# Attention with a routed expert layer on one core: transposing transfers ahead of pair loads on SyncE's queue, and products with V side by side

## The chip, the cores and the metric

The kernel runs on one core of one Trainium2 chip. The metric is device time in microseconds (us) from launch to end. Three runs of the kernel before gave 577.92, 581.92 and 582.97 us; their median is 581.92. Everything read from a trace comes from one profiled execution, which took 580.57 us and whose span from the first to the last instruction is 578.8 us.

## What is computed

Attention over 4 batches, 8 heads, 576 positions and 64 columns a head, with an additive bias that depends on the positions, then an expert layer in which each token goes to one of 8 experts.

```python
scores = scale * np.matmul(q, k.transpose(0, 1, 3, 2))
h = np.maximum(x @ w1 + b1, 0.0)          # x: 576 x 576 position ratios
bias = h @ w2                             # one 576 x 576 plane a head
scores = scores + bias.transpose(2, 0, 1)[None, :, :, :]
scores = scores - np.max(scores, axis=-1, keepdims=True)
attn = np.exp(scores)
attn = attn / (np.sum(attn, axis=-1, keepdims=True) + 1e-09)
attn_out = np.matmul(attn, v)
...
logits = np.einsum('bsd,de->bse', x, w_gate)   # x: attn_out, heads side by side
h = np.maximum(x[b, s] @ w1[e], 0.0)
out[b, s] = p[e] * (h @ w2[e])
```

## The kernel before

Two heads of one batch make a pair. There are 16 pairs (`pairs`, four head pairs p by four batches b), numbered here 0 to 15 in the order in which they run. Pairs 0 to 3 run while the bias planes are still being made; pairs 4 to 15 run one behind the other. A pair is worked in five blocks of query rows (`QORD` = 1, 2, 0, 3, 4), and a block of 128 rows in two units, one a head; the last block, of 64 rows, is one unit for both heads. So a pair has nine units, and unit u is a position in one list of events.

A unit (`emit_s`) makes a score plane on TensorE (L305, L306: the query in 16 bits against the high and the low half of the key), adds the bias and takes the minimum on VectorE (L325), and takes the exponential on ScalarE (L330). Before the product with V the exponentials have to be transposed. That goes two ways:

- For pairs 4 to 12 (`DMP`) the first two blocks are split into a high and a low 16-bit half: ScalarE casts (L336), VectorE subtracts (L346, in `emit_lo`), and a DMA turns the whole 128 x 2304 tile into `eT` (L350). There are two such transposing transfers a pair, called T1 (first block) and T2 (second block) here. `av_split` then makes the products with V, in three parts: part 0 (L363 and eight of L369) reads what both T1 and T2 brought, parts 1 and 2 are eight and eight more of L369.
- All other blocks are transposed on TensorE (L398) and copied out of PSUM (L404, L415).

VectorE's subtraction and its copies, the casts of V (L276, with a POOL subtraction behind each), the output rows (`emit_rows`: transposes L456, a scaling L468, a 16-bit cast `xo` L482 on ScalarE, its low half on POOL or VectorE) and their stores (`store_rows`, L492 and L495) lie between.

Loads: `load_pair` (L141, L143 twice, L145) brings query, key halves and V of the pair after the next one, 288 to 320 KB each, and POOL splits them into 16-bit halves (L122, L119). `load_bias` (L166 to L168 for a full block) reads the bias planes of the next head pair back from DRAM. All of them, T1, T2 and the row stores are issued by SyncE (SP), one behind the other: an instruction there that waits holds all that stand behind it. `xo` has one buffer, so the cast of a pair's rows waits until the rows before are stored.

What sets the order: each step has a key, a unit number plus a fraction (`at(u + ..., ...)`), and the steps are recorded by key. Every engine but SyncE is then ordered by a scheduler from what was recorded; in the stretch of pairs 4 to 12, SyncE keeps the recorded order word for word (`manual_schedule`). The keys that matter: a unit's work at u; T1 at the third unit of a pair and T2 at its fifth (`unit_r` at u + 0.1, which issues row stores first); the pair load at the first unit (inside `prefetch`); the bias read-backs at the fifth unit, ahead of T2; row stores `LST` = 5 units after the rows were made; `av_split`'s three parts 5.8, 8.55 and 8.8 units behind the second block's first head's end (`LA0`).

Of the kernel before, what the change touches and what calls it, by code (L numbers as in the profile page):

```python
# [21 lines left out]
NQ = 5  # L22
NP = H // 2
# [26 lines left out]
def build(tc, nc, io):  # L50
# [214 lines left out]
    dmx = ExitStack()  # L265
    dbox = {}
    pend, ucur = [], [0]
    stores, LST = [], 5

    def prefetch(gi):  # L270
        p, b, qt = groups[gi]
        if (p, b) in DMP and qt == QORD[0]:
            if "e" not in dbox:
                open_right()
            v16 = dbox["v"].tile([128, 2, NQ, 128], F16, name="v16")
            nc.vector.tensor_copy(out=v16[:, 0], in_=v_t[b, p])  # L276
            sub_pool(v16[:, 1], v_t[b, p], v16[:, 0])
            v16_t[p, b] = v16
        if p == 0:
            if G0 - 6 <= gi < G0 - 1:  # L280
                load_bias(1, QORD[gi - G0 + 6])
            if G0 - 6 <= gi < G0 - 4:
                load_pair(gi - (G0 - 6), 1, wr_t[KORD[-1]])
        else:
            if qt == QORD[0]:
                nx = gi // NQ + 2
                if nx < len(pairs):
                    load_pair(pairs[nx][1], pairs[nx][0])
            if p + 1 < NP and qt == QORD[2]:
                for x in (((0, 1), (2,), (3,), (4,)) if p < NP - 2 else ((0, 1, 2), (3, 4), (), ()))[b]:  # L290
                    load_bias(p + 1, QORD[x])

    def emit_s(u):
        gi, hh = units[u]
# [343 lines left out]
    bias_step(12)  # L638
    LB0, LC0, LO0 = 3.2, 6, 1.28
    LTS = (3.2, 3.2, 2.95, 3.2, 3.95)  # L640
    LA0, LAN, LA1, LL, LOUT = (5.8, 8.55, 8.8), 10.62, (6.35, 6.6), 8.6, 8.72
    NU = len(units)
    ex_t = {}

# [396 lines left out]
            bias_step(BSTEP[s])  # L1041

    def unit_r(s):
        while stores and stores[0][0] <= s:
            store_rows(*stores.pop(0)[1:])
        while pend and pend[0][0] < s:
            emit_lo(pend.pop(0)[1])

    def unit_x(s):
        for st in steps:  # L1050
# [26 lines left out]
    def at(key, f, *a):  # L1077
        ev.append((key, len(ev), partial(f, *a)))

    for u in range(NU):  # L1080
# [3 lines left out]
        at(u + 0.1, unit_r, u)  # L1084
        at(u + (LB0 if p == 0 else LTS[QORD.index(qt)]), emit_t, u)
        at(u + 0.4, unit_x, u)
        if qt == QORD[1] and hh == 1:
            if (p, b) in DMP:
                for n in range(3):
                    at(u + LA0[n], av_split, p, b, n)  # L1090
            elif p:
                at(u + LAN, emit_av, p, b, 0)
            else:
                at(u + LC0 + 0.6, emit_av, p, b, 0)
# [430 lines left out]
```

## Time and profile before

| | |
|---|---|
| median of three runs | 581.92 us (577.92 to 582.97) |
| the profiled execution | 580.57 us, span 578.8 us |
| TensorE matmul busy | 529.8 us, 92% of the span |
| VectorE busy | 470.5 us, 81% |
| ScalarE busy | 437.1 us, 76% |
| GpSimd (POOL) busy | 263.2 us, 45% |
| mean granted TensorE clock | 0.978 of full speed |
| HBM read, written | 128.92 MB, 20.80 MB |

How to read it: a busy share is an average over stages with different limits. Score reads of pair 4 begin at about 127 us and those of pair 13 at about 277 us; the first 127 us are the bias planes with pairs 0 to 3, the stretch from 340 us on is the expert layer. The change touches the stretch between 127 and 277 us above all. A row of the timeline merges like instructions that follow each other; the bracket gives the idle time before and what ended it. SyncE's rows give the time that an issue took, not the transfer.

### The profile page before, as it was taken

To read this page: it belongs to the slowest core of one execution; us is meant where nothing else is said; L and a number is where in the kernel's file an instruction comes from. 1 tells how busy PE (TensorE), PEld (TensorE's weight loads), DVE (VectorE), ACT (ScalarE), POOL (GpSimd) and SP (SyncE) were. 2 spreads that over 40 slices of the span, in tenths; PEclk is the share of its full clock that TensorE was granted. 3 is DMA by queue.
4 is the path that set the end of the run, shared out by engine and by line. 5 is a ranking of instruction groups with operands and counts; after the bars stand their busy time and mean duration, and the time that the engine had idled before them with its cause. 6 is when DMAs were issued, how large, how long until landed. Compare 5 with 4: busy or idle time off the path is not lost. (4 is left out here: it accounts for less than half of the span.)

```text
span 578.8 us, 14244 instructions
## 1 busy us (share of the span) xinstructions
PE 529.8 (92%) x5310; PEld 355.9 (61%) x5310; DVE 470.5 (81%) x915; ACT 437.1 (76%) x743; POOL 263.2 (45%) x293
## 2 busy tenths in 40 slices
PE   5669999989979999998999998999999999999992
PEld 1124445766646667766576776587676867777851
DVE  6989885688778898899788458789999799897950
ACT  5879876867878887887589874468998787986940
POOL 5200000894299958967646660522424354344111
PEclk9899999999989999999799999899999999999997
DMA  8766546857798799749174001776899947887250
GB/s 281 259 186 185 144 132 189 267 147 155 192 238 224 190 264 242 198 104 261 33 252 134 22 22 35 257 236 211 271 266 301 333 136 213 160 217 230 18 185 30
DMA packets 104285, 107.33 MB, mean 185 GB/s; under 512 B 71565, under 2 KB 80911, under 8 KB 100114
## 3 DMA queue, kind: packets, MB, share of 16 engines
q1 hardware_dynamic: 99424, 90.63, 56.5%
q0 software_dynamic: 4640, 15.43, 8.8%
q8 instruction: 44, 0.72, 0.5%
q10 hardware_dynamic: 146, 0.30, 0.2%
q14 instruction: 31, 0.25, 0.1%
HBM read 128.92 MB, written 20.80 MB: 259 GB/s over the span
## 5 line engine op out<-in xcount | busy, mean ns | idle before, releaser
L325 DVE CUSTOM_DVE_ANT_0 e<-sps,wb 128x576 f32<-128x576 f32 x144 | 106.8, 747 | 20.0 <-PE sps L306 15.0
L330 ACT ACTIVATE e<-e,st 128x576 f32<-128x576 f32 x144 | 111.5, 775 | 14.2 <-DVE st L325 12.7
L917 DVE TENSOR_TENSOR w<-wb,w 128x2048 bf16<-128x2048 f32 (+1 forms) x36 | 72.3, 2052 | 2.0 <-ACT w L910 2.0
L305 PE MATMUL sps<-kh,qs 128*128 128x288 f16 x256 | 69.5, 293 | 3.3 <-DVE st L325 2.8
L1014 POOL DMA_INDIRECT out_dram<-y,odx x17 | 32.2, 1892 | 88.8 <-ACT y L1004 48.8
L404 ACT COPY eT<-ta 128x512 f32<-128x512 f32 x92 | 52.6, 581 | 23.5 <-PE ta L398 16.6
L398 PE MATMUL ta<-c_cpb,e 128*128 128x128 f32 x432 | 68.1, 278 | 2.0 <-ACT eT L404 1.1
L306 PE MATMUL sps<-kl,qs 128*128 128x288 f16 x256 | 69.2, 291 | 0.0
L988 PE MATMUL yp<-w,hhT 128*128 128x512 bf16 (+1 forms) x272 | 64.9, 381 | 1.1 <-ACT w L910 1.1
L910 ACT CAST w<-wb 128x2048 f16<-128x2048 f32 (+1 forms) x40 | 63.8, 1640 | 2.2 <-DMA wb<-in_w_dram 2.2
L211 PE MATMUL sps<-hd,c_cpa 128*32 128x512 f32 (+17 forms) x352 | 48.3, 505 | 15.1 <-DVE hd L197 10.3
L949 PE MATMUL sps<-xT,we 128*128 128x128 f16 (+1 forms) x1056 | 61.3, 219 | 1.0 <-DVE we L917 1.0
L949 PEld LDWEIGHTS <-we 128*128 128x128 f16 (+1 forms) x1056 | 59.9, 98 | 3.5 <-DVE we L917 1.1
L398 PEld LDWEIGHTS ta<-c_cpb,e 128*128 128x128 f32 x432 | 50.1, 141 | 12.7 <-ACT e L330 2.6
L428 PE MATMUL av<-eT,vt 128*64 128x320 f32 (+1 forms) x368 | 57.7, 425 | 0.0
L197 DVE TENSOR_SCALAR hd<-tab,bp 128x448 f32<-128x448 f32 (+17 forms) x130 | 50.2, 445 | 3.9 <-PE sps L211 3.8
L917 DVE TENSOR_TENSOR we<-ws,we 128x2048 bf16<-128x2048 f32 (+1 forms) x25 | 49.0, 1993 | 2.7 <-ACT we L910 2.6
L949 PEld LDWEIGHTS <-wb 128*128 128x128 f16 (+1 forms) x1056 | 46.9, 98 | 2.8 <-issue 1.5
L949 PE MATMUL sps<-xT,wb 128*128 128x128 f16 (+3 forms) x1056 | 48.5, 207 | 0.0
L988 PEld LDWEIGHTS <-hhT 128*128 128x128 f16 x272 | 25.9, 99 | 30.3 <-issue 2.8
L910 ACT CAST we<-ws 128x2048 f16<-128x2048 f32 (+1 forms) x26 | 41.4, 1637 | 2.1 <-DMA ws<-in_w_dram 2.1
L119 POOL TENSOR_TENSOR qs<-qf,qs 64x288 f16<-64x288 f32 x48 | 40.9, 871 | 1.7
(234 smaller groups left out, 1008.7 us busy)
## 6 DMA issues: line engine op xcount, KB each, us to landing
ws<-in_w_dram SPq DMA_DIRECT2D x34, 1024.0 KB
wb<-in_w_dram SPq DMA_DIRECT2D x34, 1024.0 KB
hs<-in_w_dram SPq DMA_DIRECT2D x20, 1024.0 KB
bias_d<-bv SPq DMA_DIRECT2D x36, 295.5 KB
kf<-in_kt_dram SPq DMA_DIRECT2D x24, 288.0 KB
wb<-bias_d SPq DMA_DIRECT2D x16, 288.0 KB
wb<-bias_d SPq DMA_DIRECT2D x16, 256.0 KB
xrow_d<-xo SPq DMA_DIRECT2D x16, 256.0 KB
```

The lines of the kernel that those rows point to most:

```text
L197: nc.vector.tensor_scalar(out=hd[:, 0:n], in0=tab[:, 0:n], scalar1=bp[:, k:k + 1], scalar2=0.0, op0=ALU.add, op1=ALU.max,)
L305: nc.tensor.matmul(out=ps[:, half, 0:288], lhsT=lq, rhs=kh[:, j], start=True, stop=False)
L306: nc.tensor.matmul(out=ps[:, half, 0:288], lhsT=lq, rhs=kl[:, j], start=False, stop=True)
L325: nc.vector.tensor_tensor_reduce(out=e, in0=ps[:, :, 0:288], in1=bsl, scale=-0.125, scalar=1e30, op0=ALU.add, op1=ALU.min, accum_out=st[:, ...
L330: nc.scalar.activation(out=e, in_=e, func=AF.Exp, scale=-1.0, bias=st[:, 0:1], accum_out=sm)
L398: nc.tensor.transpose(out=ta[:, j, :], in_=e[:, o:o + 128], identity=ident)
L404: nc.scalar.copy(out=eTv[:, :, hh, o:o + 128], in_=ta)
L428: nc.tensor.matmul(out=av[64 * x:64 * x + 64, 0:n], lhsT=vt[:, j, 64 * x:64 * x + 64], rhs=eT[:, 2 * j + x, 0:n], start=False, stop=(j == 3),)
L910: nc.scalar.copy(out=wh[c][:, sl], in_=src)
L917: nc.vector.tensor_tensor(out=wl[c][:, sl], in0=src, in1=wh[c][:, sl], op=ALU.subtract)
L949: nc.tensor.matmul(out=hp.rearrange("p a j -> p (a j)")[:, n * f:n * f + n], lhsT=w[f // 4][:, o:o + 128], rhs=x[:, kt], start=(i == 0), s ...
L988: nc.tensor.matmul(out=yp, lhsT=x[:, kt], rhs=w[kt // 4][:, 512 * (kt % 4):512 * (kt % 4) + 512], start=(i == 0), stop=(i == len(terms) - 1),)
```

## The change

Names of constants move (`LST`, `LBI`, `LPD`, `LPN`, `LPX`), and these keys with them:

- `load_pair` leaves `prefetch` and becomes a step of its own, `load_ahead`. For the first six pairs of the stretch (pairs 4 to 9, `DMP[0:LPX]`) its key is 4.15 units behind the pair's first unit, which is behind T2; for the others it is 0.01 ahead of the first unit.
- the bias read-backs (`load_next_bias`) get key 4.2 instead of 4.0, behind T2 and behind the pair load;
- row stores come one unit later (`LST` 6), and within a unit behind the transposing transfers, not ahead of them;
- `av_split`'s parts get 7.2, 8.0 and 8.02 instead of 5.8, 8.55 and 8.8: part 0 later, parts 1 and 2 earlier and one directly behind the other.

No instruction is added or taken away on the compute engines, and no transfer.

```diff
--- before.py
+++ after.py
@@ -265,7 +265,7 @@
     dmx = ExitStack()
     dbox = {}
     pend, ucur = [], [0]
-    stores, LST = [], 5
+    stores = []
 
     def prefetch(gi):
         p, b, qt = groups[gi]
@@ -281,14 +281,16 @@
                 load_bias(1, QORD[gi - G0 + 6])
             if G0 - 6 <= gi < G0 - 4:
                 load_pair(gi - (G0 - 6), 1, wr_t[KORD[-1]])
-        else:
-            if qt == QORD[0]:
-                nx = gi // NQ + 2
-                if nx < len(pairs):
-                    load_pair(pairs[nx][1], pairs[nx][0])
-            if p + 1 < NP and qt == QORD[2]:
-                for x in (((0, 1), (2,), (3,), (4,)) if p < NP - 2 else ((0, 1, 2), (3, 4), (), ()))[b]:
-                    load_bias(p + 1, QORD[x])
+
+    def load_ahead(gi):
+        nx = gi // NQ + 2
+        if nx < len(pairs):
+            load_pair(pairs[nx][1], pairs[nx][0])
+
+    def load_next_bias(p, b):
+        if p + 1 < NP:
+            for x in (((0, 1), (2,), (3,), (4,)) if p < NP - 2 else ((0, 1, 2), (3, 4), (), ()))[b]:
+                load_bias(p + 1, QORD[x])
 
     def emit_s(u):
         gi, hh = units[u]
@@ -638,7 +640,9 @@
     bias_step(12)
     LB0, LC0, LO0 = 3.2, 6, 1.28
     LTS = (3.2, 3.2, 2.95, 3.2, 3.95)
-    LA0, LAN, LA1, LL, LOUT = (5.8, 8.55, 8.8), 10.62, (6.35, 6.6), 8.6, 8.72
+    LA0, LAN, LA1, LL, LOUT = (7.2, 8.0, 8.02), 10.62, (6.35, 6.6), 8.6, 8.72
+    LST, LBI = 6, 4.2
+    LPD, LPN, LPX = 4.15, -0.01, 6
     NU = len(units)
     ex_t = {}
 
@@ -1041,10 +1045,10 @@
             bias_step(BSTEP[s])
 
     def unit_r(s):
+        while pend and pend[0][0] < s:
+            emit_lo(pend.pop(0)[1])
         while stores and stores[0][0] <= s:
             store_rows(*stores.pop(0)[1:])
-        while pend and pend[0][0] < s:
-            emit_lo(pend.pop(0)[1])
 
     def unit_x(s):
         for st in steps:
@@ -1084,6 +1088,9 @@
         at(u + 0.1, unit_r, u)
         at(u + (LB0 if p == 0 else LTS[QORD.index(qt)]), emit_t, u)
         at(u + 0.4, unit_x, u)
+        if p and hh == 0 and qt == QORD[0]:
+            at(u + (LPD if (p, b) in DMP[0:LPX] else LPN), load_ahead, gi)
+            at(u + LBI, load_next_bias, p, b)
         if qt == QORD[1] and hh == 1:
             if (p, b) in DMP:
                 for n in range(3):
```

Three places show what it does to the order. Line numbers of the changed kernel are two higher in these places.

SyncE, from the row stores in pair 5 on; `e_1933` and `e_1967` are the tiles of T1 and T2 of pair 5, `qf`, `kf`, `vt` are the load of pair 7, `wb_126` the read-back of a bias block. Before:

```order
L492 DMA xrow_d<-xo 128x4x128
L495 DMA xrow_d<-xo 64x128
L492 DMA xrow_d<-xo 128x4x128
L495 DMA xrow_d<-xo 64x128
L141 DMA qf<-in_qt_dram 128x576
L143 DMA kf<-in_kt_dram 128x576 x2
L145 DMA vt<-in_vl_dram 128x640
L350 DMA_TRANSPOSE eT<-e_1933 128x18x128
L166 DMA wb_126<-bias_d 128x576
L167 DMA wb_126<-bias_d 128x512
L168 DMA wb_126<-bias_d 128x64
L350 DMA_TRANSPOSE eT<-e_1967 128x18x128
```

and in the changed kernel, where the same two tiles are named `e_1898` and `e_1952`:

```order
L494 DMA xrow_d<-xo 128x4x128
L497 DMA xrow_d<-xo 64x128
L494 DMA xrow_d<-xo 128x4x128
L497 DMA xrow_d<-xo 64x128
L352 DMA_TRANSPOSE eT<-e_1898 128x18x128
L352 DMA_TRANSPOSE eT<-e_1952 128x18x128
L141 DMA qf<-in_qt_dram 128x576
L143 DMA kf<-in_kt_dram 128x576 x2
L145 DMA vt<-in_vl_dram 128x640
L166 DMA wb_126<-bias_d 128x576
L167 DMA wb_126<-bias_d 128x512
L168 DMA wb_126<-bias_d 128x64
```

The load of four transfers and the three read-backs, which stood ahead of T1 and between T1 and T2, now stand behind both; the two row stores still stand ahead of T1.

VectorE, at the same place: `e_1933` and `e_1967` as above, `xo` the low half of the rows whose store is the second pair of `xrow_d` rows above; each pair of ISA rows is one unit's score read. Before:

```order
L125 TENSOR_TENSOR xo<-xr,xo 128x5x128
L382 COPY xt<-av 128x256
L415 COPY eT<-tb_r 128x64
L325 ISA e,st<-sps,wb_127 128x576
L325 ISA st 128x1
L346 TENSOR_TENSOR e_1933<-e,e_1933 128x1152
L325 ISA e,st<-sps,wb_127 128x576
L325 ISA st 128x1
L325 ISA e,st<-sps,wb_127 128x576
L325 ISA st 128x1
L346 TENSOR_TENSOR e_1967<-e,e_1967 128x1152
L442 COPY xt<-av 128x320
```

and in the changed kernel:

```order
L348 TENSOR_TENSOR e_1898<-e,e_1898 128x1152
L327 ISA e,st<-sps,wb_127 128x576
L327 ISA st 128x1
L327 ISA e,st<-sps,wb_127 128x576
L327 ISA st 128x1
L125 TENSOR_TENSOR xo<-xr,xo 128x5x128
L327 ISA e,st<-sps,wb_127 128x576
L327 ISA st 128x1
L444 COPY xt<-av 128x320
L348 TENSOR_TENSOR e_1952<-e,e_1952 128x1152
L446 COPY sums<-av 64x2
```

T1's subtraction moved ahead by one score read, and the `xo` subtraction went from ahead of both to between them.

TensorE, in pair 6, around the products of pair 5 (`v_1898` before, `v_1886` now, is V of pair 5 in 16 bits). Before, these rows hold no product with V; the first of them, L363, comes behind sixteen more rows:

```order
L414 MATMUL tb_r<-c_cpb,e 128x128
L305 LDWEIGHTS qs
L305 MATMUL sps<-kh,qs 128x288
L306 LDWEIGHTS qs
L306 MATMUL sps<-kl,qs 128x288
L305 LDWEIGHTS qs
L305 MATMUL sps<-kh,qs 128x288
L306 LDWEIGHTS qs
L306 MATMUL sps<-kl,qs 128x288
L398 MATMUL ta<-c_cpb,e 128x128 x4
L305 LDWEIGHTS qs
```

and in the changed kernel, from the same `tb_r` row on:

```order
L416 MATMUL tb_r<-c_cpb,e 128x128
L307 LDWEIGHTS qs
L307 MATMUL sps<-kh,qs 128x288
L308 LDWEIGHTS qs
L308 MATMUL sps<-kl,qs 128x288
L365 LDWEIGHTS v_1886
L365 MATMUL av<-eT,v_1886 128x256
L365 LDWEIGHTS v_1886
L365 MATMUL av<-eT,v_1886 128x256
L365 LDWEIGHTS v_1886
L365 MATMUL av<-eT,v_1886 128x256
```

Part 0 of `av_split` moved ahead by two and a half score planes here, although its key is later: the scheduler sets what it takes to be ready.

## Rows read from the trace of the kernel before

**Rows 1.** Windows view: us, busy of each engine, PEclk, DMA share, GB/s

```profile
127.00:277.00 150.00, 138.77 (x1186) 96.01 (x1185) 128.88 (x332) 119.67 (x277) 112.49 (x127) 0.98 0.81 203
```

**Rows 2.** Waits view of PE, 125 to 285 us: total us, times, longest

```profile
PE av L363 <- DMA eT<-e: 6.0, 3, 3.4
```

**Rows 3.** Timeline of PE: start us, us, line, operation [idle before <-what ended it]

```profile
147.39 0.49 PE L363 MATMUL av<-eT,v 128*128 128x256 f16 x3 [1.39 <-DMA eT<-e]
...
160.96 0.29 PE L306 MATMUL sps<-kl,qs 128*128 128x288 f16 x1
...
166.76 0.49 PE L363 MATMUL av<-eT,v 128*128 128x256 f16 x3 [3.35 <-DMA eT<-e]
...
222.32 1.30 PE L536 MATMUL av<-c_cpb,xt 128*128 128x32 f32 x10 [1.40 <-DVE sums L444]
...
272.67 0.50 PE L363 MATMUL av<-eT,v 128*128 128x256 f16 x3 [1.21 <-DMA eT<-e]
...
273.56 0.51 PE L684 MATMUL sps<-ident,fk 128*16 128x128 f16 x5 [0.16 <-DVE fk L608]
```

**Rows 4.** Windows view of PE alone: busy us, PEclk, DMA share, GB/s

```profile
168.17:171.58 3.41, 3.41 (x19) 0.50 0.50 118
...
273.98:277.39 3.41, 3.07 (x19) 0.50 0.47 146
277.39:280.80 3.41, 3.41 (x21) 0.50 0.30 87
```

**Rows 5.** Timeline of SyncE's queue: start us, us taken to issue, line

```profile
140.43 4.83 SPq L350 DMA_TRANSPOSE eT<-e  x1
...
151.59 0.58 SPq L141 DMA_DIRECT2D qf<-in_qt_dram  x1
...
153.22 0.37 SPq L145 DMA_DIRECT2D vt<-in_vl_dram  x1
153.70 4.51 SPq L350 DMA_TRANSPOSE eT<-e  x1
158.26 0.57 SPq L166 DMA_DIRECT2D wb<-bias_d  x1
...
159.88 3.27 SPq L350 DMA_TRANSPOSE eT<-e  x1
...
248.95 1.77 SPq L350 DMA_TRANSPOSE eT<-e  x1
250.81 0.53 SPq L492 DMA_DIRECT2D xrow_d<-xo  x1
251.40 0.56 SPq L495 DMA_DIRECT2D xrow_d<-xo  x1
```

**Rows 6.** Timeline of DVE around pairs 5 and 9

```profile
149.75 0.82 DVE L125 TENSOR_TENSOR xo<-xr,xo 128x640 bf16<-128x640 f32 x1
...
152.19 1.35 DVE L346 TENSOR_TENSOR e<-e,e 128x1152 f16<-128x1152 f32 x1
...
154.82 1.35 DVE L346 TENSOR_TENSOR e<-e,e 128x1152 f16<-128x1152 f32 x1
...
219.23 0.77 DVE L276 CAST v<-vt 128x640 f16<-128x640 f32 x1 [2.14 <-DMA vt<-in_vl_dram]
```

**Rows 7.** Timeline of POOL: the split of one loaded pair (pair 7)

```profile
155.37 2.08 POOL L122 TENSOR_SCALAR qs<-qf 64x576 f16<-64x576 f32 x2 [12.01 <-DMA qf<-in_qt_dram]
...
161.78 2.80 POOL L119 TENSOR_TENSOR kl<-kf,kh 128x288 f16<-128x288 f32 x4
164.55 2.51 POOL L119 TENSOR_TENSOR xo<-xr,xo 128x640 bf16<-128x640 f32 x1
```

**Rows 8.** Timeline of ACT: the output row cast that waits for a store

```profile
148.37 0.72 ACT L482 CAST xo<-xr 128x640 f16<-128x640 f32 x1 [0.92 <-DMA xrow_d<-xo]
```

**Rows 9.** Timeline of PE: the first score product of pair 7

```profile
176.85 0.30 PE L305 MATMUL sps<-kh,qs 128*128 128x288 f16 x1
```

## The prediction

> **What bounds the kernel now.** Read the windows view first, for the stretch the change touches. From the first score read of pair 4 to that of pair 13 nine pairs take 150 us, 16.7 us each, and TensorE is busy for 138.8 of them, VectorE for 128.9, POOL for 112.5, with the DMA engines at 0.81 [rows 1]. So TensorE sets the pace, with 11.2 us of idle time, and VectorE, at 86%, is the next in line. Then the waits view of TensorE: 6.0 us in three waits at L363, part 0 of the products with V, for the transposed tile `eT`, by far the most for one line [rows 2]. The timeline shows where: 1.39 us for pair 4, 3.35 us for pair 5, 1.40 us in pair 10, 1.21 us for pair 12 [rows 3]. Last, the clock: behind the 3.35 us wait the granted clock is 0.50 of full speed (1.2 instead of 2.4 GHz) for 3.41 us, and behind the 1.21 us wait it is 0.50 for twice 3.41 us [rows 4]. At half clock half of such a stretch is lost: 1.70 us and 3.41 us.
>
> Why `eT` is late is read from SyncE's queue. A transposing transfer with nothing before it is issued in 1.77 us (248.95). T1 of pair 5 took 4.51 us, right behind the four transfers of a pair load (151.59 to 153.22); T2 took 3.27 us behind a bias read-back; T2 of pair 4 took 4.83 us behind six read-backs [rows 5]. VectorE had T2's tile of pair 5 ready at 154.82 + 1.35 = 156.17 [rows 6], but it was issued from 159.88 to 163.15 and TensorE got it at 166.76 [rows 3, 5]. So 3.7 us went to the queue ahead of the issue, 1.5 us to an issue longer than 1.77, and 3.6 us lie behind it.
>
> **The change part by part.**
>
> *T2 ahead of load and read-backs.* For pair 5 the queue ahead of T2 falls away: issue at 156.2, done at about 158, data 2.1 to 3.6 us later (2.1 is 147.39 less the end of T2's issue of pair 4, 140.43 + 4.83; 3.6 is 166.76 less 163.15 [rows 3, 5]), so at 160.1 to 161.6. The changed order asks for part 0 earlier, behind the half unit that ends about 161.0 in the trace before [rows 3]. That alone would leave a wait of 0 to 0.6 us. But two row stores still stand ahead of T1 in pair 5, and their `xo` subtraction now stands behind T1's subtraction and two score reads. Before it was done at 149.75 + 0.82 = 150.6, now some 3 us later; and the `xo` cast waits for the store before, which is now behind a load and six read-backs (before, it already waited 0.92 us [rows 8]). I bound what this leaves of the 3.35 us wait by 0 and 3.35 and take 1.0, nearer the low end, because T2's own subtraction comes only two reads after T1's [rows 6]. Gain 2.35 us, and 1.70 us of half clock with it: a wait of 1.39 us (pair 4) was followed by no such stretch.
>
> For pair 4, T2's tile lands some 6 us earlier than before, since six read-backs no longer go first: the whole 1.39 us goes.
>
> *V's cast in pair 9.* VectorE waited 2.14 us at 219.23 for V of pair 11 [rows 6], and behind that cast stood T2's subtraction and the sums for which TensorE waited 1.40 us at 222.32 [rows 3]. In the changed order this cast stands in pair 11 itself, so the 1.40 us go.
>
> *Pair 12.* T2 no longer has the two row stores ahead of it, 0.53 + 0.56 us of issue [rows 5], about the size of the 1.21 us wait. But next in line at L684 is a small VectorE result, for which TensorE waited at 273.56, 0.9 us after the products began [rows 3]. The stall moves to it. I take 0.2 us, and leave the two half-clock stretches behind it, 3.41 us, where they are.
>
> *`av_split`'s parts side by side.* The same 27 products a pair, at the same durations; nothing is gained but an earlier release of `eT`'s buffer for the next T1, which is not the last thing that T1 waits for in the rows. Nothing.
>
> *Pair loads later.* POOL took 164.58 - 155.37 = 9.2 us to split pair 7, starting 3.8 us after the issue at 151.59 [rows 5, 7], and the first score product of that pair came at 176.85 [rows 9]: 12.3 us to spare. With the load issued behind T2 at 158.0 (6.4 us later) and pair 7 reached 1.39 + 2.35 + 1.70 = 5.4 us earlier, 0.5 us remain. Its price lies between 0 and, if POOL first has to do the `xo` of 2.51 us that now stands ahead of the split [rows 7], 2 us. I take 0.5 us. For the read-backs, half a pair of delay is covered: a plane is needed only in the next head pair.
>
> *Row stores later.* The `xo` cast on ScalarE may wait for them: 0.92 us before [rows 8], with price 0 to 1.8 us (twice that) and 0.5 taken.
>
> Sum: 1.39 + 2.35 + 1.70 + 1.40 + 0.20 - 0.5 - 0.5 = 6.0 us. From the profiled execution's 580.57 us this gives 574.5 us. That execution lies 1.35 us under the median of 581.92; the forecast stays with the execution from which it is worked out.
>
> **A rule that speaks against it.** The issue rows say that a transposing transfer is held up by the plain transfers ahead of it: 4.83, 4.51 and 3.27 us against 1.77 [rows 5]. The Trainium skill, in DMA: Bandwidth & Descriptors, Rules for kernel authors, says that a transpose next to ordinary DMAs needs nothing. That sentence is about what is safe and has no price; taken as a rule on time, the order on the queue would not matter, which is the first rival. The rows do not agree with it as far as the issue goes; whether the data are slowed by order or by the common load, no row here settles.
>
> **The rivals.**
>
> *The order does not pay.* The DMA engines are busy at 0.81 over the stretch [rows 1]; if T2's data are late because of that load and not because of their place, the three waits at L363 stay, and only the 1.40 us of V's cast and perhaps the 1.39 us of pair 4 are gained, with 1 us of new waits: 579 us. Or the stall of pair 5 only changes its cause, from read-backs to row stores and `xo`: then 2.35 and 1.70 us are missing from my sum, 578.5 us. Against both: the issue of 1.77 us on the empty queue.
>
> *Everything pays.* Pair 5 without a wait (+1.0), pair 12 with its 1.21 us and both half-clock stretches (+1.0 + 3.41), no new waits (+1.0): 574.5 - 6.4 = 568.1 us. Against it: the VectorE result at 273.56 is bound to nothing that the change moves.
>
> *Slower: POOL becomes the pace.* The load now waits in the queue behind row stores that need POOL's `xo`, and POOL does that `xo` behind the split of the load before. One turn is 3.8 (issue to POOL) + 9.2 (split) + 2.5 (`xo`) + 1.1 (issue of the stores) = 16.6 us, and a pair takes 16.7 us now, 16 after the gain [rows 1, 5, 7]. Where a turn comes to 18 us, the five pairs 7 to 11 run 2 us late each, and one stretch of half clock follows: 580.57 - 5.4 + 10 + 1.7 = 587 us. It decides as soon as a turn is over the pair time by more than about 1 us. Against it: 16.6 us are still under the pair time of now, and the slack of the first two pairs is used up first.
>
> **How the numbers follow.** Forecast (571 to 577.5 us) 0.48; the order does not pay (577.5 to 583) 0.28; everything pays (567 to 571) 0.12; POOL becomes the pace (583 to 592) 0.12. The likeliest case gives 574.5 us. Its own range is 571 to 577.5; for 8 in 10 the range has to reach into both neighbours: 568 to 581, leaving 0.03 below and 0.17 above. About 1% is what a measurement of this kernel can tell from no change: 576.1 us on the one side of 581.92, 587.7 on the other. Faster by over 1% takes 0.40 of the forecast's chance and all of the 0.12: 0.52. Slower by over 1% takes 0.08 of the last. The rest, 0.40, is no change.
>
> **What would show it.** In the changed profile: SyncE's rows have T1 and T2 of pairs 4 to 9 next to each other, T2 with an issue near 1.8 to 2.5 us; the waits of TensorE at the first product with V for `eT` add up to under 2.5 us, from 6.0; no half-clock stretch near 168 us; no wait of VectorE for V near 219 us. The nine pairs take about 144 us instead of 150. It is wrong if T2's data are no earlier relative to its subtraction; if POOL's split of pairs 7 to 9 ends after TensorE asks for it, which would stand as waits of the score products for POOL; or if ScalarE's waits for `xrow_d` grow by more than 2 us.

## The result: slower by half a per cent, and the profile after

The changed kernel takes 583.88 us (median of 22 runs, 579.31 to 587.35) against 581.71 us for the kernel before (22 runs): a ratio of 1.0057, 95% interval 1.0035 to 1.0079. The forecast was 574.5 us, range 568 to 581; the result lies above the range. The profiled execution of the changed kernel took 583.90 us with a span of 582.1 us, against 580.57 and 578.8.

The rows that answer those of before. First the windows view of all engines for the same stretch as [rows 1] (columns as there), then of TensorE alone for the place of the old half-clock stretch and for the two new ones:

```profile
127.00:277.00 150.00, 137.97 (x1160) 93.97 (x1159) 125.41 (x320) 118.44 (x272) 108.38 (x122) 0.99 0.74 199
```

```profile
168.17:171.58 3.41, 3.41 (x24) 1.00 0.99 165
244.54:247.95 3.41, 3.41 (x18) 0.50 1.09 261
282.08:285.49 3.41, 3.41 (x20) 0.50 0.52 125
```

TensorE does less in the same 150 us (137.97 us instead of 138.77), and so does VectorE (125.41 instead of 128.88). The half clock near 168 us is gone, as forecast, but the clock is 0.50 at 244.54 and at 282.08. Now TensorE's waits (total us, times, longest), as in [rows 2], and three rows of its timeline, as in [rows 3]:

```profile
PE tb_r L416 <- DVE xr L475: 3.2, 2, 2.3
PE av L426 <- DVE eT L417: 2.0, 2, 1.5
PE ta L400 <- DVE xr L470: 2.0, 1, 2.0
PE sps L688 <- DVE fk L610: 1.6, 1, 1.6
...
PE av L365 <- DMA eT<-e: 0.5, 1, 0.5
```

```profile
161.96 0.50 PE L365 MATMUL av<-eT,v 128*128 128x256 f16 x3 [0.50 <-DMA eT<-e]
...
208.16 0.33 PE L416 MATMUL tb_r<-c_cpb,e 128*128 128x128 f32 x1 [2.34 <-DVE xr L475]
...
242.81 0.63 PE L400 MATMUL ta<-c_cpb,e 128*128 128x128 f32 x4 [2.02 <-DVE xr L470]
```

The 6.0 us of waits for the transposed tile are 0.5 us (L363 of before is L365 now); the first product with V of pair 5 comes at 161.96 instead of 166.76. In their place stand waits for `xr`, the scaled output rows that VectorE writes: 3.2 and 2.0 us. Why VectorE is late with `xr` is in its own rows, and in POOL's, which [rows 7] showed before:

```profile
207.22 0.69 DVE L470 TENSOR_TENSOR xr<-ta,sums 128x512 f32<-128x512 f32 x1 [3.36 <-POOL xo L119]
...
216.19 0.93 DVE L276 CAST v<-vt 128x640 f16<-128x640 f32 x1 [1.69 <-DMA vt<-in_vl_dram]
...
241.97 0.69 DVE L470 TENSOR_TENSOR xr<-ta,sums 128x512 f32<-128x512 f32 x1 [2.55 <-POOL xo L119]
```

```profile
188.62 1.41 POOL L119 TENSOR_TENSOR xo<-xr,xo 128x640 bf16<-128x640 f32 x1
...
194.71 1.41 POOL L122 TENSOR_SCALAR qs<-qf 64x576 f16<-64x576 f32 x2 [3.33 <-DMA qf<-in_qt_dram]
...
202.75 3.09 POOL L119 TENSOR_TENSOR kl<-kf,kh 128x288 f16<-128x288 f32 x4
205.79 1.40 POOL L119 TENSOR_TENSOR xo<-xr,xo 128x640 bf16<-128x640 f32 x1
```

VectorE stands 3.36 us before it may write `xr` at 207.22, and 2.55 us at 241.97, because POOL has not yet read the old `xr` (the subtraction into `xo`, L119). POOL has that subtraction behind the split of a loaded pair, and the split waits for its load: 3.33 us of idle time at 194.71. From the end of one `xo` subtraction (188.62 + 1.41 = 190.03) to the end of the next (205.79 + 1.40 = 207.19) it is 17.2 us. SyncE's queue, as in [rows 5], closes the circle:

```profile
157.70 2.42 SPq L352 DMA_TRANSPOSE eT<-e  x1
160.16 0.57 SPq L141 DMA_DIRECT2D qf<-in_qt_dram  x1
...
171.15 1.86 SPq L352 DMA_TRANSPOSE eT<-e  x1
...
174.31 0.58 SPq L141 DMA_DIRECT2D qf<-in_qt_dram  x1
...
187.41 1.83 SPq L352 DMA_TRANSPOSE eT<-e  x1
190.05 0.38 SPq L494 DMA_DIRECT2D xrow_d<-xo  x1
...
191.04 0.58 SPq L141 DMA_DIRECT2D qf<-in_qt_dram  x1
...
207.21 0.39 SPq L494 DMA_DIRECT2D xrow_d<-xo  x1
...
208.21 0.58 SPq L141 DMA_DIRECT2D qf<-in_qt_dram  x1
...
232.02 7.54 SPq L143 DMA_DIRECT2D kf<-in_kt_dram  x2
```

T2 is issued in 2.42, 1.86 and 1.83 us. The row stores (L494) stand right behind it and start at 190.05 and 207.21, within 0.02 us of the end of POOL's `xo`; the next load (L141) follows the stores by 1 us. So load, split, `xo`, store and the next load form one loop. It closes twice in this profile: SyncE's stores wait for POOL's `xo` two times, 3.8 us in all. The last row is another matter: a load that sits 7.54 us in the queue. Here TensorE has no wait for `eT` behind it.

### The profile page after: what moved, and what is told of

It is laid out like the page before. It is cut to its first block, busy times and chain, and to the rows that moved or that the text cites. A ratio compares the mean times of both kernels' runs of the same rounds, so it can differ in the third digit from the quotient of the medians.

```text
span 582.1 us, 14238 instructions
## 1 busy us (share of the span) xinstructions
PE 532.0 (91%) x5310; PEld 356.0 (61%) x5310; DVE 472.6 (81%) x915; ACT 437.9 (75%) x743; POOL 259.9 (45%) x293
## 5 line engine op out<-in xcount | busy, mean ns | idle before, releaser
L1018 POOL DMA_INDIRECT out_dram<-y,odx x17 | 30.7, 1808 | 94.8 <-ACT y L1008 58.2
L406 ACT COPY eT<-ta 128x512 f32<-128x512 f32 x92 | 52.6, 580 | 18.4 <-PE ta L400 11.4
L430 PEld LDWEIGHTS av<-eT,vt 128*64 128x64 f32 x368 | 25.1, 136 | 25.2 <-issue 8.7
```

What stands on the lines that cost most here:

```text
L406: nc.scalar.copy(out=eTv[:, :, hh, o:o + 128], in_=ta)
L430: nc.tensor.matmul(out=av[64 * x:64 * x + 64, 0:n], lhsT=vt[:, j, 64 * x:64 * x + 64], rhs=eT[:, 2 * j + x, 0:n], start=False, stop=(j == 3),)
```

## The experiments

Each was timed beside the kernel before on its chip; the ratio is to that. The last columns come from VectorE's timelines: the time from the first score read of pair 4 to that of pair 10, and from pair 10 to pair 13, in the one profiled execution. The three profiles of one program (e1, f4, g4) differ there by up to 1.8 us, so smaller differences in these columns say nothing.

| kernel | us | ratio, 95% interval | pairs 4 to 9 | pairs 10 to 12 |
|---|---|---|---|---|
| before | 581.71 | 1 | 99.1 | 51.0 |
| changed | 583.88 | 1.0057 [1.0035, 1.0079] | 100.0 | 54.1 |
| h2, changed again | 583.11 | 1.0041 [1.0008, 1.0073] | 100.0 | 54.2 |
| e1, loads early | 577.22 | 0.9925 [0.9894, 0.9956] | 96.6 | 50.0 |
| f4, the same as e1 | 576.16 | 0.9903 [0.9865, 0.9940] | 97.3 | 50.0 |
| g4, the same as e1 | 575.12 | 0.9886 [0.9836, 0.9936] | 95.5 | 51.2 |
| e4, before, loads late | 590.81 | 1.0156 [1.0114, 1.0198] | 98.5 | 60.0 |
| f1, e1 with products as before | 579.98 | 0.9974 [0.9943, 1.0004] | 96.2 | 52.2 |
| f2, before, products as changed | 582.20 | 1.0033 [1.0007, 1.0060] | 96.8 | 52.9 |
| e3, load ahead of stores | 583.20 | 1.0011 [0.9981, 1.0041] | 96.9 | 55.7 |
| f3, `xo` on VectorE | 581.31 | 1.0009 [0.9974, 1.0045] | 93.5 | 58.0 |
| g1, f3 without the seam | 577.18 | 0.9910 [0.9875, 0.9945] | 93.9 | 50.0 |
| g2, changed without the seam | 587.68 | 1.0114 [1.0070, 1.0159] | 98.8 | 52.3 |
| g3, e1 with `xo` on VectorE | 579.99 | 0.9978 [0.9949, 1.0007] | 98.1 | 52.3 |
| e2, two `xr` | 588.28 | 1.0120 [1.0075, 1.0164] | 103.2 | 51.7 |
| i2, e2, one V cast later | 590.10 | 1.0139 [1.0096, 1.0183] | 98.7 | 61.5 |
| h1, e3 without the seam | 585.28 | 1.0051 [1.0014, 1.0087] | 97.0 | 56.5 |
| i1, h1, one V cast later | 584.42 | 1.0050 [1.0019, 1.0081] | 98.0 | 54.3 |
| j1, i1 with two `xo` | 583.04 | 1.0038 [1.0013, 1.0062] | 97.2 | 53.7 |
| j2, j1 with two `xr` | 582.39 | 1.0037 [1.0005, 1.0068] | 97.0 | 52.2 |

### Which part costs: the loads (e1, e4, and f4 and g4)

e1 is the changed kernel with the loads of all pairs back at the pair's head; e4 is the kernel before with the late loads alone.

```diff
-    LPD, LPN, LPX = 4.15, -0.01, 6
+    LPD, LPN, LPX = 4.15, -0.01, 0      # e1
+    LPD, LPN, LPX = 2.05, -0.01, 6      # f4
+    LPD, LPN, LPX = 2.05, -0.01, 9      # g4
```

```diff
             if qt == QORD[0]:                            # before.py, prefetch
+            if qt == QORD[0] and (p, b) not in DMP[0:6]:  # e4
...
+        if hh == 0 and qt == QORD[0] and (p, b) in DMP[0:6]:
+            at(u + 4.15, load_ahead, gi)
```

> The changed kernel with one part undone: all pair loads stand at the head of their pair again, as before; T1 and T2 adjacent, row stores and read-backs later, products with V at 7.2, 8.0, 8.02 stay. Theory P (the late load makes POOL start its split late, POOL's output-row subtraction behind it frees the one xr tile late, VectorE waits for it in order, and TensorE behind VectorE): POOL's 30.5 us of waits for loaded queries falls to about 20, VectorE's 7.1 us of waits for POOL's output-row subtraction to under 3, and 4 to 6 us come back: 578 to 580 us, against 583.9 for the changed kernel and 581.7 for the one before. Theory V (the later, bunched products with V are the cost: VectorE gets its scores late and then all at once): nothing changes, 583 to 585 us. Theory S (the later row stores are the cost): 583 to 585 us as well.

> The kernel before with one part of the change alone: the loads issued in pairs 4 to 9 stand 4.15 units later, all else as before (row stores ahead of T1, read-backs ahead of T2, products with V at 5.8, 8.55, 8.8). Theory P: POOL starts each split some 6 us later, and the time grows by 2 to 5 us to 584 to 587 us, with VectorE waits for POOL's output-row subtraction as in the changed kernel. Theory V: no loss from loads alone, and T1 of these pairs no longer stands behind a load: 579 to 582 us.

> The changed kernel with the pair loads of pairs 4 to 9 two units later than the head of the pair instead of four, so ahead of T1 and T2, which stay next to each other. A load is some 3 us earlier than in the changed kernel and some 3 us later than in e1. Theory P as a matter of slack (POOL had about 2 to 3 us to spare, all lateness beyond it is paid): close to e1, 577 to 579.5 us. Theory loop through the stores (load behind stores is what costs): also 577 to 579.5 us, since the load stands ahead of the stores that wait for the split. If each unit of lateness costs the same: half way, 580 to 581.5 us.

> The kernel of f4 with loads two units late in all nine pairs 4 to 12. The seam there is small (a late load of pair 9 and an early one of pair 10 lie some 11 us apart): theory seam says next to nothing, 575 to 577.5 us. If early loads in pairs 10 to 12 are worth something of their own: 578 to 580 us.

f4 and g4 were meant to put the loads half as late, and did not: 2.05 lies ahead of the step that issues T1, as -0.01 does, and SyncE has nothing between the two. All five engines got the same instructions in the same order as in e1. So e1 was measured three times, 0.9925, 0.9903 and 0.9886, mean 0.9905 (5.5 us less than the kernel before), and nothing is known of a half-late load.

The changed kernel, measured twice (1.0057, and 1.0041 as h2), has the mean 1.0049. The later loads therefore cost 0.0144 x 581.8 = 8.4 us, with what the scheduler makes of their new keys on the other engines, and e4, the late loads alone, says 9.1 us. Theory V (the products) and theory S (the stores) are out: with products and stores as changed, e1 is faster. By stage the cost in the changed kernel is 3.5 us in pairs 4 to 9 (100.0 us against 96.5, the mean of the three profiles of e1) and 3.8 us in pairs 10 to 12 (54.2 against 50.4). In e4 it is all in pairs 10 to 12 (60.0 against 51.0 before), and VectorE never waits for POOL's subtraction there, which the expectation had named as the sign: e4 shows the cost of late loads, but not by that way. What it shows is the seam, which comes below.

In e1 VectorE's waits for POOL's `xo` subtraction, 7.1 us in the changed kernel, are gone. TensorE's waits in the same stretch are small, and none is for `xr`:

```profile
PE sps L307 <- DVE st L327: 2.0, 5, 1.0
PE tb_r L414 <- DVE eT L417: 1.9, 3, 0.9
...
PE av L365 <- DMA eT<-e: 0.2, 1, 0.2
```

> The changed kernel itself, beside h1 on one chip: 583 to 585 us by every theory.

### What is left without the late loads (f1, f2)

f1 is e1 with `LA0 = (5.8, 8.55, 8.8)`; f2 is the kernel before with `LA0 = (7.2, 8.0, 8.02)`.

> The kernel of e1 (changed kernel with the pair loads at the head again, 577.2 us against 581.8 before) with the products with V also back at 5.8, 8.55, 8.8: what is left of the change is SyncE's order, T2 ahead of the bias read-backs and T1, T2 ahead of the row stores. Theory Q (T1 and T2 next to each other on the queue bring the gain): 577 to 579 us. Theory V (the gain comes from asking for the tile later, at 7.2): 581 to 583 us, with over 3 us of waits of TensorE for the transposed tile.

> The kernel before with the products with V alone at 7.2, 8.0, 8.02; loads, stores and read-backs stand as before. Theory V: TensorE's 6.0 us of waits for the transposed tile fall to 2 or 3, since it asks later, and the time falls to 577 to 579 us. Theory Q: the tile is as late as before and something else waits for it; 580.5 to 582.5 us.

SyncE's order alone gives 0.9974, which its interval does not set apart from no change, the products alone 1.0033, both 0.9905. Neither theory holds by itself: f1 at 580.0 us lies between the two ranges, f2 at 582.2 us in that of theory Q, and only both together gain. In f1 TensorE still waits 2.3 us for the transposed tile, in f2 2.2 us; with both it is 0.2 us in the rows of e1 above. Why the products alone lose 0.3%, where the waits they aim at fall from 6.0 to 2.2 us, is not settled.

### The loop and the seam (e3, f3, g1, g2)

The seam is the place where the last late load (of pair 9) meets the first early one (of pair 10). `LPX` sets how many pairs load late: 6 in the changed kernel, 9 without a seam. e3 puts the load between T2 and the row stores, f3 moves the `xo` subtraction from POOL to VectorE:

```diff
         while pend and pend[0][0] < s:            # e3, unit_r
             emit_lo(pend.pop(0)[1])
+
+    def unit_w(s):
         while stores and stores[0][0] <= s:
...
         at(u + 0.1, unit_r, u)
+        at(u + 0.18, unit_w, u)
```

```diff
-        (sub_dve if on_act and ... else sub_pool)(lo, xr, hi)
+        (sub_dve if (p, b) in DMP or on_act and ... else sub_pool)(lo, xr, hi)   # f3
```

> The changed kernel with the pair load between T2 and the row stores instead of behind the stores: it is as late as in the changed kernel by the order on the queue, but no longer waits for POOL's output-row subtraction of the pair before. Theory P with the loop (load waits for stores, stores for the subtraction, the subtraction for the split of the load before): POOL's waits for loaded queries fall by 1 to 2 us in each of five pairs, the turn of POOL drops from about 17 to about 15 us, and the time falls by 2 to 5 us to 579 to 582 us. If only the place of the load in time counts and not the loop: 583 to 584 us. Theory V: 583 to 585 us.

> The changed kernel with the output-row subtraction of pairs 4 to 12 on VectorE instead of POOL: the row stores and with them the load behind them no longer wait for POOL, and xr comes free without POOL; VectorE takes nine subtractions of 0.82 us more, 7.4 us. Theory loop (load waits for stores, stores for POOL's subtraction, that for the split of the load before): loads are issued right behind T2, POOL's turn shrinks by about 2 us in pairs 7 to 11, the new waits of TensorE fall by 4 us or more, and after paying part of VectorE's 7.4 us the time is 579 to 582 us. If lateness of the load alone, without the loop, is the cause: 583 to 586 us. If VectorE becomes the pace: above 586 us.

> The kernel of f3 (output-row subtraction on VectorE, 581.3 us) with the loads late in all nine pairs 4 to 12 instead of the first six, so that no late load (of pair 9) is followed at once by an early one (of pair 10). In f3 that second load sat in SyncE's queue for 7.52 us at 226.91, T1 and T2 of pair 10 behind it, and TensorE waited 5.3 us for the transposed tile. Theory seam (the two loads next to each other are the second loss): this wait goes, with it two half-clock stretches, 575 to 578 us. Against it, loads late for pairs 12 to 14 as well: if their own lateness costs as much, 580 to 583 us.

> The changed kernel with the loads late in all nine pairs 4 to 12: the loop through POOL stays, the seam goes (there the load sat for 7.54 us at 232.02). Theory loop plus seam, both of a size: 580 to 582.5 us, 1.5 to 4 us below the changed kernel. If the loop is nearly all: 583 to 586 us, with the turn of 17 us going on into pairs 10 to 12.

g2 shows the loop longest, since there no early load ends it. These are POOL's rows for the first step of each split:

```profile
177.31 1.41 POOL L122 TENSOR_SCALAR qs<-qf 64x576 f16<-64x576 f32 x2 [1.25 <-DMA qf<-in_qt_dram]
...
194.57 1.41 POOL L122 TENSOR_SCALAR qs<-qf 64x576 f16<-64x576 f32 x2 [3.45 <-DMA qf<-in_qt_dram]
...
211.46 1.41 POOL L122 TENSOR_SCALAR qs<-qf 64x576 f16<-64x576 f32 x2 [1.20 <-DMA qf<-in_qt_dram]
...
228.55 1.41 POOL L122 TENSOR_SCALAR qs<-qf 64x576 f16<-64x576 f32 x2 [3.06 <-DMA qf<-in_qt_dram]
...
245.67 1.41 POOL L122 TENSOR_SCALAR qs<-qf 64x576 f16<-64x576 f32 x2 [0.95 <-DMA qf<-in_qt_dram]
...
262.42 1.41 POOL L122 TENSOR_SCALAR qs<-qf 64x576 f16<-64x576 f32 x2 [3.00 <-DMA qf<-in_qt_dram]
```

The turns are 17.3, 16.9, 17.1, 17.1 and 16.8 us, and POOL idles 1 to 3.5 us for the load in each. This is the pace of the kernel there: VectorE's waits for `xo` come to 8.5 us in five, TensorE's behind it to 6.0, and SyncE's stores wait for it in five pairs:

```profile
SPq L494 <- POOL xo L119: 6.9, 5, 2.6
```

Cutting the loop speeds up the first six pairs, as the loop theory says: from 100.0 us to 96.9 with the load ahead of the stores (e3) and to 93.5 with the stores free of POOL (f3, which also takes 1.4 us of work a pair off POOL). Both give it back in pairs 10 to 12, 55.7 and 58.0 us against 54.1. So f3 at 581.31 us lies in the range of theory loop, but e3 at 583.20 us in that of its rival, by which only the place of the load in time counts. In e3 TensorE's longest wait in pairs 10 to 12 is one of 3.05 us for a score read (at 232.43), as in h1 below. In f3 it is the seam:

```profile
220.18 0.59 SPq L141 DMA_DIRECT2D qf<-in_qt_dram  x1
...
226.28 0.34 SPq L141 DMA_DIRECT2D qf<-in_qt_dram  x1
226.91 7.52 SPq L143 DMA_DIRECT2D kf<-in_kt_dram  x2
...
235.01 7.30 SPq L352 DMA_TRANSPOSE eT<-e  x2
```

```profile
244.97 0.82 PE L365 MATMUL av<-eT,v 128*128 128x256 f16 x3 [5.31 <-DMA eT<-e]
```

The load that pair 10 issues comes 6.1 us behind that of pair 9. `kf` has three buffers and a load takes two, so the second key half of the later load gets one only when POOL has split the first key half of the earlier one: POOL ends there at 234.07, and the transfer is issued at 234.10. The two halves together hold the queue for 7.52 us, T1 and T2 of pair 10 wait behind it, and TensorE stands 5.31 us. e4 has the same, worse:

```profile
228.31 10.84 SPq L143 DMA_DIRECT2D kf<-in_kt_dram  x2
```

```profile
249.49 0.82 PE L366 MATMUL av<-eT,v 128*128 128x256 f16 x3 [5.35 <-DMA eT<-e]
```

Without the seam, g1 is at 577.18 us, 1.0% below f3, with 50.0 us for pairs 10 to 12. In the changed kernel, where the loop stays, taking the seam away (g2) gains 3 us up to pair 13 (151.1 instead of 154.1 us) and loses them again behind it, where the loads for pairs 12 to 14 are now late too: pair 13 takes 22.1 us instead of 19.9, pair 14 21.4 instead of 18.0. Both ranges expected for g2 missed its 587.68 us. Its profiled execution, 583.66 us, is the fastest of its six, so 4.0 us of what it loses in the median are in no profile.

### Where the lateness comes out (e2, i2, h1, i1, j1, j2)

e2 gives the changed kernel a second `xr`, and changes nothing in the order of any engine's work, one early memset aside; h1 is e3 without the seam; i1 and i2 hold back VectorE's cast of V of one pair; j1 and j2 add a second `xo`, then also a second `xr`, to i1:

```diff
+        dbox["x"] = dmx.enter_context(tc.tile_pool(name="xr2", bufs=1, side="right"))
+        dbox["xr"] = dbox["x"].tile([128, NQ, 128], F32, name="xr2")
...
     def emit_rows(p, b, u):
+        xr = dbox["xr"] if (p, b) in DMP[0:8] and b % 2 else xr1      # e2, j2; xo alike in j1, j2
...
+            with tc.issue_after(dbox["ttr"].ins) if (p, b) == DMP[7] else ExitStack():  # i1; DMP[6] in i2
+                nc.vector.tensor_copy(out=v16[:, 0], in_=v_t[b, p])
```

> The changed kernel with a second xr tile (the scaled rows) for every other pair of 4 to 11, so that VectorE may write the next pair's rows while POOL still reads the last ones; nothing moves on any queue. Theory P with xr as the link: VectorE's 7.1 us of waits for POOL's output-row subtraction vanish, with them the 5.2 us that TensorE waited behind them (3.2 and 2.0), and the time falls by 3 to 5 us to 579 to 581 us. If POOL's lateness reaches TensorE by another way (the score products of the next pair, the stores and behind them T1): 582 to 584 us with waits of TensorE for POOL or for the transposed tile in their place. Theory V: 583 to 585 us.

> The kernel of e3 (loads still behind T2, but ahead of the row stores; POOL does the same work as in the changed kernel) with the loads at that place in all nine pairs 4 to 12, so without the seam. Theory loop: POOL's turn, 17.1 us with the loop, drops under 16 us in pairs 8 to 11, and the time to 576 to 581 us. Theory POOL's work (its 12 to 13 us a pair are too much for any late load): turns stay at 17 us and the time at 584 to 588 us, as in g2.

> The kernel of h1 with one instruction held back: VectorE's cast of V of pair 11 stands behind the last score read of pair 10 instead of in the middle of pair 10. SyncE's queue is the same, instruction by instruction. Theory cast (the late load costs a second time where VectorE casts V in order): the waits of 1.67 us on VectorE and 3.59 us on TensorE go, with them two half-clock stretches (3.4 us), and the time falls by 4 to 7 us to 578 to 581 us. If the cast only showed a lateness that comes out elsewhere: 583.5 to 586 us, with a new wait in pair 10 or 11.

> The kernel of e2 (two xr tiles) with VectorE's cast of V of pair 10 behind the last score read of pair 9. Theory cast: pair 9 takes 17 us instead of 24.0, without the 5.72 us wait and the three half-clock stretches behind it, and the time falls by 5 to 8 us to 580 to 583 us, the seam in pair 10 still being there. If only moved: 586 to 589 us.

> The kernel of i1 with a second xo tile (output rows before their store) for every other pair of 4 to 11, so ScalarE need not wait for the store of the pair before. SyncE's queue is the same. Theory of single tiles: ScalarE's 5.7 us of waits for row stores fall under 1.5, TensorE's 5.2 us behind ScalarE under 2, and the time falls by 3 to 6 us to 578.5 to 581.5 us. If xr then holds VectorE instead: 582 to 585 us with over 4 us of VectorE waits for POOL's subtraction.

> The kernel of j1 with a second xr tile too: no single tile is left between the late load and TensorE but the loaded tiles themselves. Theory of single tiles: 576 to 580 us, near g1 (577.2 us), with loads as late as in h1. If late loads cost in yet another way: 582 to 586 us.

e2 refutes `xr` as the one link. VectorE's waits for POOL's `xo` are gone and the kernel is slower by 4 us, because the lateness comes out at two other places in pair 9. SyncE, VectorE, ScalarE and TensorE there:

```profile
211.63 0.42 SPq L145 DMA_DIRECT2D vt<-in_vl_dram  x1
```

```profile
216.91 1.02 DVE L276 CAST v<-vt 128x640 f16<-128x640 f32 x1 [5.72 <-DMA vt<-in_vl_dram]
```

```profile
211.66 0.72 ACT L485 CAST xo<-xr 128x640 f16<-128x640 f32 x1 [5.01 <-DMA xrow_d<-xo]
```

```profile
213.67 0.66 PE L400 MATMUL ta<-c_cpb,e 128*128 128x128 f32 x4 [3.07 <-ACT eT L406]
...
218.12 1.44 PE L426 MATMUL av<-eT,vt 128*128 128x320 f32 x2 [1.34 <-DVE eT L417]
```

The row stores start at 208.47, when POOL's `xo` has ended (208.45). ScalarE's next cast into `xo` stands 5.01 us for them, since `xo` is single too, and TensorE 3.07 us behind ScalarE. V of pair 10 is issued at 211.63, behind the same stores; VectorE's cast of it stands 5.72 us, and TensorE 1.34 us behind VectorE. TensorE's clock is 0.50 from 214.25 to 224.49.

h1 has neither loop nor seam (POOL's turns are 16.3, 15.3, 16.9 and 17.7 us, where under 16 was expected), and is no faster than the changed kernel beside it (585.28 us against 583.11 for h2, on one chip), nor than e3, which has the seam. A cast of V, of pair 11, costs it time:

```profile
232.97 0.75 DVE L276 CAST v<-vt 128x640 f16<-128x640 f32 x1 [1.67 <-DMA vt<-in_vl_dram]
```

```profile
236.24 0.40 PE L307 MATMUL sps<-kh,qs 128*128 128x288 f16 x1 [3.59 <-DVE st L327]
```

Behind that cast stand a subtraction and the score read for which TensorE waits 3.59 us. Holding back the cast takes these waits away (i1), and then ScalarE waits for the row stores, 5.7 us instead of 4.4, with TensorE behind it:

```profile
ACT xo L485 <- DMA xrow_d<-xo: 5.7, 6, 2.3
```

```profile
PE av L431 <- ACT eT L405: 5.2, 4, 2.1
```

In i2 pair 9 falls from 24.0 to 18.4 us as expected, but the time does not fall (590.10 us against 588.28): ScalarE's waits for row stores grow from 7.3 to 9.8 us, and a load sits 8.45 us in the queue at the seam, with a wait of 4.28 us for `eT` on TensorE behind it. From h1 over i1 and j1 to j2 the stretch from pair 4 to pair 13 shrinks in every profile, 153.5, 152.3, 150.9, 149.2 us. The ratios do not show it: 1.0051 to 1.0037, with intervals that cover each other almost wholly. So a gain of the second tiles is not shown.

In none of these six did the theory named first in its expectation hold by its time. h1 lies in the range of theory POOL's work, i1, j1 and j2 in those of their rivals, e2 and i2 above all ranges. j1's rival had a sign, waits of VectorE for POOL's subtraction over 4 us, and has none of them. j2 does not reach the 576 to 580 us that the theory of single tiles expected. Up to pair 13 it takes 2.3 us more than e1, f4 and g4 on average (146.9), and behind it 4 us more, with VectorE waiting for no load longer than 0.4 us. What that rest is stays open. The orders of the other engines differ between h1, i1 and j1, since only SyncE's is written out by hand, and that was not separated.

g3 asked whether the `xo` subtraction on VectorE is worth something by itself:

> The kernel of f4 (loads two units late, ahead of T1 and T2, 576.2 us) with the output-row subtraction on VectorE as in f3. In f4 POOL's subtraction no longer stands in TensorE's way (no wait of VectorE for it over 0.5 us in pairs 4 to 12), so theory loop says there is nothing to gain here: 7.4 us of VectorE work more, of which a part shows, 576 to 580 us. If POOL's subtraction still costs there: 572 to 575 us.

It is not: with 0.9978 against 0.9905 it costs 4.2 us, of the 7.4 us that VectorE has to do more.

Set beside g1, g3 says something else too. Both have that subtraction on VectorE, both ran on one chip, and they differ in the loads: late in all nine pairs in g1, early in g3. There the late loads are the faster ones, 0.9910 [0.9875, 0.9945] against 0.9978 [0.9949, 1.0007]. So late loads do not cost by themselves, as far as two kernels show it whose other engines are ordered differently too. They cost where POOL has the `xo` subtraction to do behind their split, and at the seam. Whether it is the order of that subtraction or POOL's 1.4 us for it that counts is not separated, since f3 and g1 take both away.

The fastest kernels of the study are e1, the change without the later loads, with 0.9905 of the kernel before over its three measurements, and g1 with 0.9910; the runs do not tell them apart.

## Why the prediction was wrong

**T2 ahead of load and read-backs (3.74 us, and 1.70 us of half clock): right in kind.** The waits for `eT` are 0.5 us, T2's issue takes 1.78 to 2.50 us, the half clock near 168 us is gone, and the first score read of pair 7 comes 48.1 us after that of pair 4 instead of 51.0. That is 2.9 us of the forecast 5.4 (0.8 to 2.6 us in the three profiles of e1); a part of the rest stands as waits for VectorE's copies into `eT` at L426, 2.0 us in two, and not all of it is accounted for. The rule weighed there, of the Trainium skill, DMA: Bandwidth & Descriptors, Rules for kernel authors, that a transpose next to ordinary DMAs needs nothing, does not carry over to time: T2 of pair 5 was issued in 3.27 us behind a read-back [rows 5] and in 2.42 us behind T1, and its data were there 161.96 - 160.12 = 1.8 us after the issue, not 3.6.

**V's cast (1.40 us): right for that pair only.** The prediction lists these 1.40 us at 222.32 among the waits for `eT`, in pair 10; the row in [rows 3] is a wait for `sums`, in pair 9, and the three waits for `eT` are the other three. The sum has it once, so it does not change. The wait at 219.23 [rows 6] went, and another stands at 216.19 (1.69 us), for a load that is late itself.

**Pair 12 (0.20 us): the stall moved as forecast, the clock did not stay.** In the changed kernel TensorE waits 1.6 us at L688 (L684 of before) for the small VectorE result, and one of the two half-clock stretches is left (282.08). In all three profiles of e1 both are gone, which the forecast gave to the rival in which everything pays.

**Without the loads' term the sum was 6.0 + 0.5 = 6.5 us; e1 gains 5.5.** The total is about right, but in part by luck: the first score read of pair 7 shows 0.8 to 2.6 us of the 5.4 forecast for T2, and the half-clock stretches behind pair 12, which the forecast left where they were, make up for some of what is missing.

**Pair loads later (0.5 us, bounds 0 and 2): the step that failed; it measured 8.4 us.** Three errors are in it. First, when the load is issued: I added the delay of T2's place, 6.4 us. The load of pair 5 came at 160.16 instead of 151.59, 8.6 us later, and the next at 174.31, 14.1 us behind its pair's first score read, where before it stood 3.4 us behind (163.2 less 159.8). T2 itself waits for VectorE's subtraction of the pair, so all that is put behind T2 waits with it. Second, whom the split makes wait: I measured the slack to the first score product of the loaded pair, 12.3 us [rows 7, 9]. That slack held: in the changed kernel no score product waits for POOL. But POOL works in order, and the `xo` subtraction behind the split had no such slack (VectorE waits 7.1 us for it, in three pairs): `xr`, `xo`, the row stores and, behind them, the next load hang on it. Third, I took the price once and not for each pair.

**The rival "POOL becomes the pace" (0.12) is what happened in pairs 4 to 9, and not the whole of it.** Of the 8.4 us, 3.5 lie there and 3.8 in pairs 10 to 12, where h1's profile loses as much without the loop (56.5 us). Its turn was 3.8 + 9.2 + 2.5 + 1.1 = 16.6 us; measured are 17.2 us in the changed kernel and 16.8 to 17.3 in g2, with 1.0 for the stores' issue, 3.7 from load to POOL, 11.1 for the split and 1.4 for `xo`. The 9.2 us of [rows 7] were the shortest split in the trace, not a usual one: pair 8's took 9.8 us and pair 9's 11.0 before. Against it I argued that 16.6 is under the pair time of 16.7; but the gain was to bring that to 16, so by my own numbers the loop would have been the bound. Its 587 us is 3 us too much, although it leaves out the seam, which the limit of six pairs puts into the change; that it came so near is luck, since more than half of the loss lies elsewhere. It had the wrong signs, too: I looked for score products waiting for POOL and for ScalarE's waits for stores to grow by over 2 us (1.2 us measured, 1.7 before), not for VectorE at `xr`.

**Row stores later (0.5 us): not seen.** ScalarE's waits for stores are 1.2 us, 1.7 before, and e1, with the later stores, gains.

## What to carry to other kernels

When a transfer is moved back in a queue, read when the instruction that it now follows becomes ready, not how many places it moves; then list everything that stands behind its consumer on the consumer's engine, and ask if one of these releases the very queue that the transfer stands in. If so there is a loop, and its turn, made of usual durations and not of the shortest, has to be well under the pace that the change is to reach. Where single tiles lie between two in-order engines, taking one wait away can move the lateness to the next tile (e2, i1); moving the transfer forward (e1), or taking the step that links the two off the engine between them (g1), did more here.

## What the runs showed of the hardware

Waits of other engines can cost TensorE more than the time that it stands, through its clock. In e2 TensorE had little to do while ScalarE stood for a store and VectorE for V (columns as in [rows 4]):

```profile
210.83:214.25 3.42, 0.58 (x4) 1.00 0.88 248
214.25:217.66 3.41, 2.52 (x13) 0.50 0.99 351
```

From 214.25 on the granted clock was 0.50 (1.2 instead of 2.4 GHz) in three stretches, 10.2 us in a row, of which half is lost, 5.1 us; TensorE's own waits in that pair were 3.07 and 1.34 us. The length of a wait does not tell it: in the changed kernel the wait of 2.34 us at 208.16 was followed by no half clock, that of 2.02 us at 242.81 was, from 244.54 on.

VectorE's cast of V (128 x 640, to 16 bits) takes twice as long in the changed kernel as in e1 (columns: operation and count, then least/median/most in ns, first and last start; the changed kernel first):

```profile
L276 DVE CAST v<-vt x8: 421/934/1353, 124.6 to 252.2; 128x640 f16<-128x640 f32 x8
```

```profile
L276 DVE CAST v<-vt x8: 424/482/494, 126.8 to 238.2; 128x640 f16<-128x640 f32 x8
```

Late loads alone do not do it: in g2, with the loads late too, the median is 0.49 us. The cast at 216.19 in the changed kernel took 0.93 us. Just before it POOL had begun a cast of its own:

```profile
216.10 1.54 POOL L122 TENSOR_SCALAR kh<-kf 128x576 f16<-128x576 f32 x2
```

That row holds two POOL instructions, the first of which ended 0.59 us after 216.19; VectorE's cast ended 0.34 us behind that. The casts of 0.42 to 0.49 us in e1 began when POOL was idle or within 0.1 us of the end of an instruction. The Trainium skill, SBUF — State Buffer, Who interferes with whom, says that a cast on VectorE can take a pair of ports that it shares with GpSimd, and that whoever starts first holds it for the whole instruction while the other blocks. These rows agree with it. What it costs in all was not measured; as an estimate, 0.45 us (the difference of the two medians) for each of nine casts is about 4 us of VectorE's time.
